# Attention and a mixture of experts on one core: GpSimd's drain alone ahead of the last branch, landings awaited inside the hand-ordered program, and the downward steps in another order

## The chip, the cores and the metric

The kernel runs on one core of a Trainium2 chip. The metric is the device time of one execution in microseconds (us). Before the change it is 524.77 us, the median of 3 runs (524.23 to 525.05). The core's engines are named as in the profile: PE (TensorE) does matmuls and transposes, DVE (VectorE) and ACT (ScalarE) do elementwise work and reductions, POOL (GpSimd) does some copies and generates the indirect DMAs, SP (SyncE) issues the other DMAs. PEld is PE's loading of weights, which overlaps its matmuls.

## What is computed

Attention, then a mixture of experts, on B = 4 sequences of S = 768 tokens with H = 8 heads of 64:

```python
keep = (pos < n_global) | ((rel >= 0) & (rel < n_local))     # 8 and 96
scores = where(keep, q @ k.T / 8 - slope[h] * dist, -1e9)
a = softmax(scores);  x = (a @ v) as 3072 rows of 512
logits = x @ w_gate;  expert = argmax(logits);  gate = softmax(logits)[expert]
for e in range(8):
    h = maximum(x[expert == e] @ w1[e], 0)                    # 512 x 1024
    out[expert == e] = gate * (h @ w2[e])                     # 1024 x 512
```

## The kernel before, in words

**One program in a written order.** Every operation is first recorded by a `Flow` in the order in which the code calls it. `derive` works out, per engine, which semaphores each operation has to wait for: an operation waits for the last writers of what it reads, for the readers of what it overwrites, and, in PSUM, bank by bank, for any other engine's last touch of that bank. `play` (L192) then emits all of it, engine by engine in the recorded order, as one block `tile_critical(name="flow")` (L207). There is no planner: the order of the calls is the order on each engine. Each DMA queue entry has a semaphore (`RINGS`); `play` collects their last levels in `landed`, and SP awaits them at the end of the block (L223-224). Stores to the output are left out of that (`later=outs`, in `rest`): they are awaited at the very end of the kernel (from L1668).

**Attention** (the first 170 us) runs over 24 blocks of 128 tokens. Each token's row, with its gate and its index, is scattered by GpSimd (L602) into a region of its expert in DRAM.

**The experts** (from 169.9 us) follow in the order 0, E, 1 to 7, by `group(p)`; E is a small extra region of tokens of expert 0 that came late. For each expert the tokens are padded to one of 17 widths (`SIZES`, 128 to 256 columns for half of the tokens); PE chooses the form of its code by a switch on a loaded index (`emit_forms`), by a branch (L260) that a hint some way ahead announces (L240). The two matrix products are each done in seven block products instead of eight: `up` is two times seven steps of 8 matmul records, `down` is seven steps of 16. A step of `down` takes 1.85 us in group 7 (136 columns) and up to 2.81 us in groups 1 and 5 (208 columns).

**The seven steps** are in `seven`. They use three PSUM banks X, Y and W out of `sets = ((0, 1, 2), (3, 4, 7))`, and the set changes with every call. `one` puts a product in X, and ACT copies it out as p1 (L833). `two` puts one in Y, and DVE adds it to p1 as u2 (L837). `three` adds a product to X and ACT takes c11 from it. `four` writes Y again, DVE makes u3 = u2 + Y (L848). `five` writes W and DVE makes c22 = u3 + W (L852); `six` writes Y and DVE makes c21 = u3 + Y (L857); `last` adds a product to W, and DVE makes c12 = u2 + W (L862). In `down` these four results are the quarters of the expert's output, transposed: c11 and c12 are blocks 0 and 2 of the tokens, c21 and c22 are blocks 1 and 3.

**Steps have numbers.** `up` has 0 to 13, `down` 14 (`D`) to 20. `at_(i, ...)` hangs other work behind the step number i: the sums of the next expert's weights (L683-686, `w_sums`) and inputs (L779, `x_in`), the issue of weight DMAs, the padding scatters (L728).

**The output of a group** is made by `y_out` (L790): four PE transposes into bank 6 or 5 (L794), a scale by the gate on ACT (L797) or on DVE (L799), and an indirect store that GpSimd generates (L800). It is called for the group before, between the first steps of `up`. Only the last group has none behind it: its four `y_out` (blocks 1, 3, 0, 2) come when all steps are done.

**The check and the end.** Behind the step D + 1 of the last group `check` (L1134) computes whether the inputs are such that this fast program is right: DVE reduces the sums of the softmax to one number per partition (L1139-1141), PE transposes it (L1143), DVE combines it with other conditions into `flag`. Behind the flow's block all engines load the flag (L1663) and branch on it (L1665): `anything` is a slow version for all inputs, and it isn't taken here. The flow's block ends with a drain of GpSimd, which stands in the trace at L207. `anything` has a wait of its own for the output stores (`again`).

Of the kernel before, what the change touches and what calls it, by code (L numbers as in the profile page):

```python
# [24 lines left out]
class Flow:  # L25
# [163 lines left out]
            op["clock"] = clock  # L189
        return procs  # L190

    def play(self, later=()):  # L192

        procs = self.derive()
        ops, tc = self.ops, self.tc
        sems = {p: tc.alloc_semaphore(f"{p[0].lower()}{'' if p[1] is None else p[1]}") for p in procs}
        level = {p: 0 for p in procs}
        landed, rest = {}, {}
        for op in ops:
            if op["dma"]:  # L200
                level[op["proc"]] += 16
                late = any(isinstance(t, str) and t in later for t in op["w"])
                (rest if late else landed)[op["proc"]] = level[op["proc"]]
            elif op.get("told"):
                level[op["proc"]] += 1
            op["level"] = level[op["proc"]]
        with tc.tile_critical(name="flow"):  # L207
            k = 0
            while k < len(ops):
                form = ops[k]["form"]  # L210
                if form is None:
                    self.emit(ops[k], sems, None)
                    k += 1
                    continue
                body = []
                while k < len(ops) and ops[k]["form"] is form:
                    if ops[k]["e"] == "PE":
                        body.append(ops[k])
                    else:
                        self.emit(ops[k], sems, None)  # L220
                    k += 1
                self.emit_forms(form, body, sems)
            for p, v in landed.items():  # L223
                self.nc.sync.wait_ge(sems[p], v)
        return [(sems[p], v) for p, v in rest.items()]

    def wait(self, op, sems):
        for j in op["need"]:
# [71 lines left out]
class Attention:  # L300
# [9 lines left out]
    GW, LW, P, E = 32, 97, 128, 8  # L310
# [299 lines left out]
class Experts:  # L610
# [9 lines left out]
    P, E, CAP, LATE = 128, 8, 512, 128  # L620
# [182 lines left out]
            _r=[k["to"][:, g, j:j + 1], self.y[j]], _w=[f"out{g}.{j}"])  # L803


    def product(self, bank, w, x, fresh):

        f, n = self.f, len(w)
        for t in range(2):
            for k in range(n):  # L810
                f.pe.matmul(self.psum[:, bank, 256 * t:256 * t + 256], lhsT=w[k][:, ts(t, 128)], rhs=x[k],  # L811
                            start=(fresh and t == 0 and k == 0), stop=True, skip_group_check=True, _dyn=True)

    def seven(self, c, a, s, cols, order, dst, act):

        f, V = self.f, self.f.dve
        X, Y, W = self.sets[self.turn]
        p1, u2, u3 = self.p1[self.turn], self.u2[self.turn], self.u3[self.turn]
        self.turn ^= 1

        def bank(b):
            return self.psum[:, b, :].rearrange("p (t c) -> p t c", t=2)

        def mm(b, wq, xq, fresh):
            self.product(b, [c[wq][:, k, cols] for k in order], [xq[:, k, :] for k in order], fresh)

        def relu(d):
            if act:
                f.act.activation(d, d, act)  # L829

        def one():
            mm(X, "b11", a["a11"], True)
            f.act.copy(p1, bank(X))  # L833

        def two():
            mm(Y, "t2", s[1], True)
            V.tensor_tensor(u2, p1, bank(Y), ALU.add)  # L837

        def three():
            mm(X, "b21", a["a12"], False)  # L840
            if act:
                f.act.activation(dst["c11"], bank(X), act)
            else:
                f.act.copy(dst["c11"], bank(X))

        def four():
            mm(Y, "t3", s[2], True)
            V.tensor_tensor(u3, u2, bank(Y), ALU.add)  # L848

        def five():  # L850
            mm(W, "t1", s[0], True)
            V.tensor_tensor(dst["c22"], u3, bank(W), ALU.add)  # L852
            relu(dst["c22"])

        def six():
            mm(Y, "t4", a["a22"], True)
            V.tensor_tensor(dst["c21"], u3, bank(Y), ALU.add)  # L857
            relu(dst["c21"])

        def last():  # L860
            mm(W, "b22", s[3], False)
            V.tensor_tensor(dst["c12"], u2, bank(W), ALU.add)  # L862
            relu(dst["c12"])

        return [one, two, three, four, five, six, last]

    def h_sums(self, j):
        V, sh = self.f.dve, self.sh
# [17 lines left out]
            steps += self.seven(c, a, s, slice(256 * j, 256 * j + 256), (0, 1), dst, AF.Relu)  # L886
        return steps

    def down(self, e):
        c, h, yt = self.quarters(e, False), self.h, self.yt  # L890
        a = dict(a11=h[:, 0:4, 0], a12=h[:, 4:8, 0], a21=h[:, 0:4, 1], a22=h[:, 4:8, 1])
        s = [self.sh[:, j] for j in range(4)]
        dst = dict(c11=yt[:, 0:2, 0], c12=yt[:, 2:4, 0], c21=yt[:, 0:2, 1], c22=yt[:, 2:4, 1])
        return self.seven(c, a, s, slice(0, 256), (0, 1, 2, 3), dst, None)


    def plain(self, e, slack):
# [23 lines left out]
def kernel(  # L921
# [12 lines left out]
    nc = tc.nc  # L934

    P = 128
    B, H, S, D = q.shape
    DM, E = moe_w_gate.shape
# [42 lines left out]
    with ExitStack() as stack:  # L981
# [149 lines left out]
        order = [0, E, *range(1, E)]  # L1131
        forms = [(keep["index"][0:1, g:g + 1], ex.SIZES, f"form{g}") for g in range(E)]

        def check():  # L1134


            ok, den = keep["ok"], keep["den"][:].rearrange("p n h -> p (n h)")
            for j, (src, op) in enumerate(((den, ALU.min), (den, ALU.max))):
                V.tensor_reduce(ok[:, j:j + 1], src, AX.X, op)  # L1139
            V.tensor_scalar(ok[:, 2:3], ok[:, 0:1], 0.125, None, ALU.is_ge)  # L1140
            V.scalar_tensor_tensor(ok[:, 3:4], ok[:, 1:2], 1.0e12, ok[:, 2:3], ALU.is_le, ALU.mult)
            row = psum[0:1, ex.tbanks[0], 0:P]
            f.pe.transpose(row, ok[:, 3:4], ident[:])  # L1143
            V.tensor_reduce(ok[0:1, 4:5], row, AX.X, ALU.min)
            V.tensor_reduce(ok[0:1, 0:1], keep["cnt"][0:1, :], AX.X, ALU.max)
            V.scalar_tensor_tensor(ok[0:1, 1:2], ok[0:1, 0:1], float(CAP), ok[0:1, 4:5], ALU.is_le, ALU.mult)
            V.scalar_tensor_tensor(ok[0:1, 2:3], keep["cnt"][0:1, E:E + 1], float(LATE), ok[0:1, 1:2], ALU.is_le,
                                   ALU.mult)
            V.scalar_tensor_tensor(ok[0:1, 5:6], ng[0:1], float(at.GW), ok[0:1, 2:3], ALU.is_le, ALU.mult)
            V.scalar_tensor_tensor(ok[0:1, 6:7], nl[0:1], float(at.LW), ok[0:1, 5:6], ALU.is_le, ALU.mult)  # L1150
            V.scalar_tensor_tensor(ok[0:1, 7:8], nl[0:1], 1.0, ok[0:1, 6:7], ALU.is_ge, ALU.mult)
            V.tensor_scalar(keep["flag"][0:1], ok[0:1, 7:8], -1.0, 1.0, ALU.mult, ALU.add)
# [16 lines left out]
        def group(p):  # L1169
# [6 lines left out]
            def at_(i, *fns):  # L1176
                todo.setdefault(i, []).extend(fns)
# [70 lines left out]
            else:  # L1248
                if nxt is not None:
                    sums, xs = ex.w_sums(nxt, True), ex.x_sums()  # L1250
                    at_(13, lambda: ex.x_in(nxt, 0))
                    at_(D + 1, lambda: ex.x_in(nxt, 1), sums[0])
                    at_(D + 3, xs[0], xs[1])
                    at_(D + 4, sums[1])
                    at_(D + 5, sums[2])
                    at_(D + 6, xs[2], xs[3], lambda: ex.marks(nxt))
                else:
                    at_(D + 1, check)
                if after is not None:
                    pieces = ex.w_pieces(after)  # L1260
                    at_(3, lambda: ex.pads(after))
# [5 lines left out]
                return  # L1267
            with f.forms(*forms[g]):
                run(ups[3:] if p else ups[2:], 3 if p else 2)
                run(ex.down(g), D)  # L1270
            assert not todo, todo

        for p in range(len(order)):
            group(p)
        for j, on in ((1, "act"), (3, "dve"), (0, "act"), (2, "dve")):
            ex.y_out(order[-1], j, on)
        outs = {f"out{g}.{j}" for g in range(E + 1) for j in range(1 if g == E else 4)}
        landing = f.play(later=outs)


    def anything(ctx):
        wpool = ctx.enter_context(tc.tile_pool(name="wpool", bufs=2))
        nc.scalar.dma_start(out=wg[:], in_=moe_w_gate.rearrange("(c p) e -> p c e", p=P))
        with tc.tile_critical(name="again"):
            for sem, level in landing:
                nc.gpsimd.wait_ge(sem, level)
            nc.gpsimd.iota(ebase[:], pattern=[[NTOK, E]], base=0, channel_multiplier=0,
                           allow_small_or_imprecise_dtypes=True)
        nc.vector.tensor_copy(out=base_e[:], in_=ebase[:])
        nc.gpsimd.iota(tokid[:], pattern=[[P, NBLK]], base=0, channel_multiplier=1)  # L1290

# [352 lines left out]
        with tc.manual_schedule(engines={PE}):  # L1644
# [5 lines left out]
            for j in range(JT):  # L1650
# [7 lines left out]
                if j + 2 < JT:  # L1658
                    fetch(j + 2)
            down(JT - 1)  # L1660


    redo = nc.values_load(keep["flag"][0:1, 0:1], min_val=0, max_val=1,  # L1663
                          skip_runtime_bounds_check_because="a comparison's result")
    with tc.If(redo > 0):  # L1665
        with ExitStack() as stack:
            anything(stack)
    with tc.tile_critical(name="landed"):  # L1668
        for sem, level in landing:
            nc.sync.wait_ge(sem, level)  # L1670


# [28 lines left out]
```

## Time and profile before

| what | us |
|---|---|
| median of 3 runs | 524.77 |
| the profiled execution's own time | 525.96 |
| its span, from the first instruction to the last | 524.1 |
| attention, up to the first step of the experts | 0 to 169.9 |
| last matmul step of the experts ends | 501.6 |
| end of the last generated store (L800) | 508.55 |
| its landing | 509.79 |
| GpSimd's drain | 505.63 to 515.25 |
| branches on the flag | 515.9 |

Busy time in four stretches of the span (us, PE's granted clock as a share of full speed):

| stretch | PE | DVE | ACT | POOL | clock |
|---|---|---|---|---|---|
| 0 to 165 | 147.74 | 110.47 | 91.09 | 95.59 | 0.98 |
| 240 to 480 | 237.57 | 173.25 | 57.51 | 47.51 | 1.00 |
| 480 to 510 | 20.95 | 16.55 | 5.29 | 3.89 | 0.97 |
| 510 to 524.1 | 0.00 | 0.00 | 0.00 | 0.00 | 0.50 |

An engine's row in the profile gives its busy time, the mean of one instruction, and the idle time ahead of it with what ended that. The chain of waits follows the work that ended last back to the beginning. DRAIN, COMPARE_BRANCH and EVENT_SEMAPHORE are records that don't count as busy; what lies behind 508.55 us consists of them and of DMAs.

### The profile page before, as it was taken

How to read it: one execution, taken by the hardware profiler on the slowest of the kernel's cores; microseconds unless marked ns; L12 is line 12 of the kernel's file. 1: busy time of each engine (PE TensorE's matmuls, PEld its weight loads, DVE VectorE, ACT ScalarE, POOL GpSimd, SP SyncE). 2: the span in 40 equal slices, each digit the busy share in tenths (PEclk: the TensorE clock that was granted, in tenths of full speed). 3: DMA queues.
4: the chain of work that ended last, by engine and by line, in shares of the span. 5: the costliest groups of instructions: out<-in, count | busy, mean ns of one | idle time of the engine just before them, and what ended most of it. 6: DMA issues, size and time to landing. Idle time of an engine off the chain costs nothing.

```text
span 524.1 us, 10715 instructions
## 1 busy us (share of the span) xinstructions
PE 480.1 (92%) x4397; PEld 451.6 (86%) x4397; DVE 349.4 (67%) x612; ACT 173.0 (33%) x290; POOL 168.5 (32%) x194
## 2 busy tenths in 40 slices
PE   4999999999968999999999999999998999999740
PEld 3788888888857999999999998999998999999740
DVE  4554765787885882747667866876865775777620
ACT  3765555656552222123033033023022113213210
POOL 1554465676675043240043042034032012002020
PEclk9999999999997999999999999999999999999985
DMA  9999999997325439996782880782891764001010
GB/s 153 205 246 248 177 218 258 224 226 187 88 89 115 161 135 210 207 282 124 179 224 73 202 223 29 159 237 80 189 258 53 161 197 112 1 3 63 1 44 8
DMA packets 120345, 79.25 MB, mean 151 GB/s; under 512 B 86422, under 2 KB 103318, under 8 KB 120272
## 3 DMA queue, kind: packets, MB, share of 16 engines
q1 hardware_dynamic: 112960, 63.77, 55.4%
q0 software_dynamic: 6480, 14.45, 7.7%
q8 instruction: 51, 0.84, 0.7%
q14 instruction: 22, 0.18, 0.1%
q10 hardware_dynamic: 832, 0.02, 0.1%
HBM read 61.39 MB, written 23.71 MB: 162 GB/s over the span
## 4 chain that ended last, share of the span: by engine, by line
PE 81%; DVE 7%; ACT 3%; POOL 2%; issue 2%; DMA 2%; POOLq 0%; SPq 0%; DVEq 0%; ACTq 0%
PE psum L811 55%; PE psum L466 6%; PE psum L503 6%; PE psum L904 3%; PE psum L794 2%; DVE arena L476 2%; PE psum L518 2%; PE psum L442 2%; PE psum L525 2%; PE psum L450 2%; DMA arena<-in_k_dram 2%; POOL xg_dram L602 1%; DVE arena L546 1%; ACT arena L444 1%; ACT arena L484 1%
## 5 line engine op out<-in xcount | busy, mean ns | idle before, releaser
L811 PE MATMUL psum<-arena 128*128 128x208 f32 (+5 forms) x1792 | 299.3, 328 | 2.6 <-ACT arena L833 2.4
L811 PEld LDWEIGHTS psum<-arena 128*128 128x128 f32 x1792 | 288.7, 190 | 8.6 <-ACT arena L833 3.3
L800 POOL DMA_INDIRECT out_dram<-arena,to x33 | 38.4, 1163 | 239.9 <-ACT arena L797 207.2
L476 DVE TENSOR_TENSOR arena<-psum,arena 128x1024 f32<-128x1024 f32 x40 | 48.8, 1219 | 37.7 <-PE psum L466 35.3
L490 POOL TENSOR_TENSOR arena<-arena 128x512 f32<-128x512 f32 x40 | 52.9, 1322 | 32.8 <-ACT arena L484 32.8
L484 ACT ACTIVATE arena<-arena 128x1024 f32<-128x1024 f32 (+1 forms) x48 | 47.4, 987 | 47.4 <-DVE arena L476 41.5
L466 PE MATMUL psum<-arena 64*128 64x128 f32 x704 | 50.1, 290 | 3.3 <-POOL arena L1035 1.4
L466 PEld LDWEIGHTS psum<-arena 64*128 64x128 f32 x704 | 44.6, 196 | 8.2 <-issue 3.7
L829 ACT ACTIVATE arena<-arena 128x512 f32<-128x512 f32 x48 | 30.2, 630 | 64.4 <-DVE arena L852 31.9
L503 PE MATMUL psum<-arena 128*64 128x128 f32 x704 | 44.6, 279 | 0.2 <-issue 0.2
L833 ACT COPY arena<-psum 128x512 f32<-128x512 f32 x24 | 14.0, 585 | 87.2 <-PE psum L811 87.1
L503 PEld LDWEIGHTS psum<-arena 128*64 128x64 f32 x704 | 38.8, 139 | 3.3 <-issue 0.6
L848 DVE TENSOR_TENSOR arena<-arena,psum 128x512 f32<-128x512 f32 x24 | 16.5, 688 | 29.9 <-PE psum L811 25.8
L602 POOL DMA_INDIRECT xg_dram<-arena,slot_i x24 | 27.0, 1126 | 21.2 <-DVE arena L862 15.8
L728 POOL DMA_INDIRECT xg_dram<-small,pad x24 | 26.3, 1098 | 12.5 <-issue 7.0
L797 ACT ACTIVATE arena<-psum,gt 128x512 f32<-128x512 f32 x31 | 19.8, 684 | 25.7 <-PE psum L794 25.7
L862 DVE TENSOR_TENSOR arena<-arena,psum 128x512 f32<-128x512 f32 x24 | 16.5, 688 | 17.5 <-PE psum L811 16.3
L852 DVE TENSOR_TENSOR arena<-arena,psum 128x512 f32<-128x512 f32 x24 | 16.5, 688 | 16.6 <-PE psum L811 15.2
L857 DVE TENSOR_TENSOR arena<-arena,psum 128x512 f32<-128x512 f32 x24 | 16.5, 688 | 14.7 <-PE psum L811 12.0
L837 DVE TENSOR_TENSOR arena<-arena,psum 128x512 f32<-128x512 f32 x24 | 16.4, 685 | 11.4 <-PE psum L811 10.3
L442 PE MATMUL psum<-ident,arena 128*128 128x128 f32 x96 | 15.5, 286 | 7.2 <-DMA arena<-in_k_dram 7.2
L779 DVE STREAM_TRANSPOSE arena<-arena 128x1024 f32<-128x1024 f32 (+1 forms) x17 | 20.3, 1203 | 2.7 <-PE psum L904 2.6
(139 smaller groups left out, 497.3 us busy)
## 6 DMA issues: line engine op xcount, KB each, us to landing
arena<-in_moe_w_dram SPq DMA_DIRECT2D x64, 512.0 KB
arena<-xg_dram SPq DMA_DIRECT2D x64, 128.0 KB
arena<-in_q_dram SPq DMA_DIRECT2D x24, 256.0 KB
arena<-in_k_dram SPq DMA_DIRECT2D x24, 256.0 KB
arena<-in_v_dram SPq DMA_DIRECT2D x24, 256.0 KB
xg_dram<-arena SPq DMA_DIRECT2D x2, 1032.0 KB
out_dram<-arena,to POOLq DMA_INDIRECT x33
xg_dram<-arena,slot_i POOLq DMA_INDIRECT x24
```

What stands on the lines that cost most here:

```text
L442: f.pe.transpose(pt[:, m, :], raw[:, 2 * m:2 * m + 2, :].rearrange("p a d -> p (a d)"), self.keep["ident"][:])
L466: f.pe.matmul(self.psum[:, 2 * g + a, c:c + P], lhsT=kt[r, m, :], rhs=qt[r, m, :], start=True, stop=True, skip_group_check=True)
L476: f.dve.tensor_tensor(e, s, self.bias[:, g, :, 1:3, :].rearrange("p h k c -> p h (k c)"), ALU.add)
L484: f.act.activation(e, e, AF.Exp)
L490: f.pool.tensor_tensor(self.es[n % 3][:, g], e[:, :, 0:P], e[:, :, P:2 * P], ALU.add)
L503: f.pe.matmul(po[r, m, :], lhsT=self.v[(n - ab) % 6][:, 2 * m + a, :], rhs=self.e[n % 2][:, m // 2, 2 * a + m % 2, P * ab:P * ab + P], sta ...
L602: self.f.pool.indirect_dma_start(out=self.xs[:], out_offset=bass.IndirectOffsetOnAxis(ap=k["slot_i"][:, b % 2, u:u + 1], axis=0), in_=self ...
L728: self.f.pool.indirect_dma_start(out=self.xs[:], out_offset=bass.IndirectOffsetOnAxis(ap=self.keep["pad"][:, g, j:j + 1], axis=0), in_=sel ...
L779: self.f.dve.transpose(out=self.xt[:, :, hh, 0:32 * nb].rearrange("p c (b t) -> p b c t", t=32), in_=self.x[g][:, hh, 0:nb])
L800: f.pool.indirect_dma_start(out=self.out[:], out_offset=bass.IndirectOffsetOnAxis(ap=k["to"][:, g, j:j + 1], axis=0), in_=self.y[j], in_of ...
L811: f.pe.matmul(self.psum[:, bank, 256 * t:256 * t + 256], lhsT=w[k][:, ts(t, 128)], rhs=x[k], start=(fresh and t == 0 and k == 0), stop=Tru ...
L829: f.act.activation(d, d, act)
```

## The change

- `play` no longer leaves out the output's stores: all landings are awaited by SP at the end of the flow's block, in the order in which the last DMAs of the semaphores were issued. The block is made with `no_gpsimd_drain=True`, and stands in a block of the program named "fast". The waits of `again` and `landed` are gone.
- Ahead of the flag's load stand a branch hint for all engines, placed there, and a drain of GpSimd alone (`nc.gpsimd.drain()`). The `If` has the false side as its fallthrough.
- `seven` takes a function `half`. If there is one, the steps come in the order one, two, four, five, six, three, last, and `three` calls it between its two halves (`product`). `group` hands a lambda to `down` in every group; its list `early` is empty but in the last group, where it holds blocks 1 and 3. Their `y_out` so comes in the middle of `three`, and blocks 0 and 2 follow at the end.
- `check` is cut in two: the four DVE operations on the sums (`check_sums`) stay behind step D + 1, the transpose and what follows it come behind step D + 3.

In the changed file the matmuls of the steps stand at L810 (L811 before), the add behind `two` at L838 (L837 before).

```diff
             op["clock"] = clock
         return procs
 
-    def play(self, later=()):
+    def play(self):
 
         procs = self.derive()
         ops, tc = self.ops, self.tc
         sems = {p: tc.alloc_semaphore(f"{p[0].lower()}{'' if p[1] is None else p[1]}") for p in procs}
         level = {p: 0 for p in procs}
-        landed, rest = {}, {}
+        landed = {}
         for op in ops:
             if op["dma"]:
                 level[op["proc"]] += 16
-                late = any(isinstance(t, str) and t in later for t in op["w"])
-                (rest if late else landed)[op["proc"]] = level[op["proc"]]
+                landed.pop(op["proc"], None)
+                landed[op["proc"]] = level[op["proc"]]
             elif op.get("told"):
                 level[op["proc"]] += 1
             op["level"] = level[op["proc"]]
-        with tc.tile_critical(name="flow"):
+        with tc.tile_critical(name="flow", no_gpsimd_drain=True):
             k = 0
             while k < len(ops):
                 form = ops[k]["form"]
...
                 self.emit_forms(form, body, sems)
             for p, v in landed.items():
                 self.nc.sync.wait_ge(sems[p], v)
-        return [(sems[p], v) for p, v in rest.items()]
 
     def wait(self, op, sems):
         for j in op["need"]:
...
             _r=[k["to"][:, g, j:j + 1], self.y[j]], _w=[f"out{g}.{j}"])
 
 
-    def product(self, bank, w, x, fresh):
+    def product(self, bank, w, x, fresh, half=None):
 
         f, n = self.f, len(w)
         for t in range(2):
             for k in range(n):
                 f.pe.matmul(self.psum[:, bank, 256 * t:256 * t + 256], lhsT=w[k][:, ts(t, 128)], rhs=x[k],
                             start=(fresh and t == 0 and k == 0), stop=True, skip_group_check=True, _dyn=True)
-
-    def seven(self, c, a, s, cols, order, dst, act):
+            if half and t == 0:
+                half()
+
+    def seven(self, c, a, s, cols, order, dst, act, half=None):
 
         f, V = self.f, self.f.dve
         X, Y, W = self.sets[self.turn]
...
         def bank(b):
             return self.psum[:, b, :].rearrange("p (t c) -> p t c", t=2)
 
-        def mm(b, wq, xq, fresh):
-            self.product(b, [c[wq][:, k, cols] for k in order], [xq[:, k, :] for k in order], fresh)
+        def mm(b, wq, xq, fresh, half=None):
+            self.product(b, [c[wq][:, k, cols] for k in order], [xq[:, k, :] for k in order], fresh, half)
 
         def relu(d):
             if act:
...
             V.tensor_tensor(u2, p1, bank(Y), ALU.add)
 
         def three():
-            mm(X, "b21", a["a12"], False)
+            mm(X, "b21", a["a12"], False, half)
             if act:
                 f.act.activation(dst["c11"], bank(X), act)
             else:
...
             V.tensor_tensor(dst["c12"], u2, bank(W), ALU.add)
             relu(dst["c12"])
 
-        return [one, two, three, four, five, six, last]
+        return [one, two, four, five, six, three, last] if half else [one, two, three, four, five, six, last]
 
     def h_sums(self, j):
         V, sh = self.f.dve, self.sh
...
             steps += self.seven(c, a, s, slice(256 * j, 256 * j + 256), (0, 1), dst, AF.Relu)
         return steps
 
-    def down(self, e):
+    def down(self, e, half=None):
+
         c, h, yt = self.quarters(e, False), self.h, self.yt
         a = dict(a11=h[:, 0:4, 0], a12=h[:, 4:8, 0], a21=h[:, 0:4, 1], a22=h[:, 4:8, 1])
         s = [self.sh[:, j] for j in range(4)]
         dst = dict(c11=yt[:, 0:2, 0], c12=yt[:, 2:4, 0], c21=yt[:, 0:2, 1], c22=yt[:, 2:4, 1])
-        return self.seven(c, a, s, slice(0, 256), (0, 1, 2, 3), dst, None)
+        return self.seven(c, a, s, slice(0, 256), (0, 1, 2, 3), dst, None, half)
 
 
     def plain(self, e, slack):
...
         order = [0, E, *range(1, E)]
         forms = [(keep["index"][0:1, g:g + 1], ex.SIZES, f"form{g}") for g in range(E)]
 
-        def check():
+        def check_sums():
 
 
             ok, den = keep["ok"], keep["den"][:].rearrange("p n h -> p (n h)")
...
                 V.tensor_reduce(ok[:, j:j + 1], src, AX.X, op)
             V.tensor_scalar(ok[:, 2:3], ok[:, 0:1], 0.125, None, ALU.is_ge)
             V.scalar_tensor_tensor(ok[:, 3:4], ok[:, 1:2], 1.0e12, ok[:, 2:3], ALU.is_le, ALU.mult)
+
+        def check():
+            ok = keep["ok"]
             row = psum[0:1, ex.tbanks[0], 0:P]
             f.pe.transpose(row, ok[:, 3:4], ident[:])
             V.tensor_reduce(ok[0:1, 4:5], row, AX.X, ALU.min)
...
                     at_(D + 5, sums[2])
                     at_(D + 6, xs[2], xs[3], lambda: ex.marks(nxt))
                 else:
-                    at_(D + 1, check)
+                    at_(D + 1, check_sums)
+                    at_(D + 3, check)
                 if after is not None:
                     pieces = ex.w_pieces(after)
                     at_(3, lambda: ex.pads(after))
...
                 return
             with f.forms(*forms[g]):
                 run(ups[3:] if p else ups[2:], 3 if p else 2)
-                run(ex.down(g), D)
+                early = ((1, "act"), (3, "dve")) if nxt is None else ()
+                run(ex.down(g, lambda: [ex.y_out(g, j, on) for j, on in early]), D)
             assert not todo, todo
 
         for p in range(len(order)):
             group(p)
-        for j, on in ((1, "act"), (3, "dve"), (0, "act"), (2, "dve")):
+        for j, on in ((0, "act"), (2, "dve")):
             ex.y_out(order[-1], j, on)
-        outs = {f"out{g}.{j}" for g in range(E + 1) for j in range(1 if g == E else 4)}
-        landing = f.play(later=outs)
+        with tc.block(name="fast"):
+            f.play()
 
 
     def anything(ctx):
         wpool = ctx.enter_context(tc.tile_pool(name="wpool", bufs=2))
         nc.scalar.dma_start(out=wg[:], in_=moe_w_gate.rearrange("(c p) e -> p c e", p=P))
-        with tc.tile_critical(name="again"):
-            for sem, level in landing:
-                nc.gpsimd.wait_ge(sem, level)
-            nc.gpsimd.iota(ebase[:], pattern=[[NTOK, E]], base=0, channel_multiplier=0,
-                           allow_small_or_imprecise_dtypes=True)
+        nc.gpsimd.iota(ebase[:], pattern=[[NTOK, E]], base=0, channel_multiplier=0,
+                       allow_small_or_imprecise_dtypes=True)
         nc.vector.tensor_copy(out=base_e[:], in_=ebase[:])
         nc.gpsimd.iota(tokid[:], pattern=[[P, NBLK]], base=0, channel_multiplier=1)
 
...
             down(JT - 1)
 
 
+    tc.mark_branch_hint_location("redo", "LikelyTaken", list(mybir.ALL_ENGINES))
+    nc.gpsimd.drain()
     redo = nc.values_load(keep["flag"][0:1, 0:1], min_val=0, max_val=1,
                           skip_runtime_bounds_check_because="a comparison's result")
-    with tc.If(redo > 0):
+    with tc.If(redo > 0, preferred_fallthrough_block=True, label="redo"):
         with ExitStack() as stack:
             anything(stack)
-    with tc.tile_critical(name="landed"):
-        for sem, level in landing:
-            nc.sync.wait_ge(sem, level)
 
 
 # ---- launch: one core; inputs and outputs as the reference has them ----
```

## The prediction, made before the run

> **What bounds the kernel now.** I read the page's busy shares and its chain first, to see which engine carries the end; then the timeline of one turn between two downward steps; then the waits of the last 45 us; then the records behind the last transfer.
>
> ```profile
> PE 480.1 (92%) x4397; PEld 451.6 (86%) x4397; DVE 349.4 (67%) x612; ACT 173.0 (33%) x290; POOL 168.5 (32%) x194
> ...
> PE 81%; DVE 7%; ACT 3%; POOL 2%; issue 2%; DMA 2%; POOLq 0%; SPq 0%; DVEq 0%; ACTq 0%
> ...
> L811 PE MATMUL psum<-arena 128*128 128x208 f32 (+5 forms) x1792 | 299.3, 328 | 2.6 <-ACT arena L833 2.4
> ```
>
> PE is the path: 81% of the chain, and ahead of 1792 matmuls of L811 it idles 2.6 us in all. Whatever stops PE between two of these matmuls is paid in full. Now one turn, group 5 (PE, then DVE):
>
> ```profile
> 411.68 8.60 PE L811 MATMUL psum<-arena 128*128 128x208 f32 x48
> ```
>
> ```profile
> 412.83 0.69 DVE L837 TENSOR_TENSOR arena<-arena,psum 128x512 f32<-128x512 f32 x1 [0.72 <-PE psum L811]
> 413.44 1.22 DVE L686 TENSOR_TENSOR arena<-arena 128x1024 f32<-128x1024 f32 x1
> ```
>
> 48 matmuls run without a break, one every 0.176 us. Step `two` ends in them, and `three` starts at 412.56. DVE adds bank Y (L837) from 412.83 to 413.52, while PE is in bank X with `three`. In the last group PE does stop, at the check's transpose:
>
> ```profile
> PE psum L1143 <- DVE ok L1141: 2.8, 1, 2.8
> ```
>
> And the end: the four stores, and the records of lines 207 and 1665 (engine op xcount: minimum/median/maximum ns).
>
> ```profile
> 503.75 0.97 POOL L800 DMA_INDIRECT out_dram<-arena,to  x1 [27.29 <-DVE arena L799]
> ...
> 507.58 0.97 POOL L800 DMA_INDIRECT out_dram<-arena,to  x1 [0.30 <-issue]
> ```
>
> ```profile
> L207 POOLq DRAIN  x1: 9620/9620/9620, 505.6 to 505.6; - x1
> ```
>
> ```profile
> L1665 SPq EVENT_SEMAPHORE  x9: 17/17/17, 519.4 to 519.9; - x9
> ...
> L1665 PEldq COMPARE_BRANCH  x1: 4603/4603/4603, 515.7 to 515.7; - x1
> ```
>
> The last store is generated by E = 508.55 (507.58 + 0.97) and recorded as landed at 509.79. GpSimd's drain ends at 515.25; only then do the engines load the flag (0.5 us) and branch (515.9). Their next records stand at 519.1 to 520.4. The end is at 524.1: 15.55 us behind E.
>
> **Part 1, the turned order, groups 0 to 6.** `down` hands `half` to every group, and a lambda is always true, so all eight groups get the order one, two, four, five, six, three, last. That moves `three` (bank X, 16 matmul records) behind `six`, and puts `four` right behind `two`. Both write bank Y, and `four` waits for L837's read of it. Today `three` covers this read; then nothing does. In group 5 PE would go on at 412.56, L837 ends at 413.52, and a PE that waited for L837 started 0.05 behind its end at 481.50 (480.77 + 0.68 = 481.45). That is 1.01 us; the second matmul behind such a wait comes some 0.1 late (0.22 instead of 0.116 at 481.50). So 1.1 us. Groups 1 to 6 all show the same 1.01 from their own rows: 6 x 1.1 = 6.6. In group 0 the add stands behind twelve table operations (L1125 to L740) and ends at 196.68, where `three` starts at 194.83: 1.9 + 0.1 = 2.0. Sum **+8.6**. From below 0 per turn, if a write could enter the bank beside the read; from above the 2.76 of the longest PE wait on DVE. I take 1.1, since both ends of this wait are rows of the same instructions.
>
> What follows loses nothing: behind L837, DVE has L686, L779 and L683 queued (to 4.4 us after `two`), so `four`'s add comes late at 5.1, but `six`, which needs it, starts at 1.1 + 2 x 2.5 = 6.1 in the groups of 184 columns. `last` needs `five`'s add, done long before. The DMAs issued at these places (the w1 pieces behind `one`, the w2 pieces behind `last`) keep them; at the same distance to PE, they land a group ahead.
>
> [...]
>
> **Part 2, the last group.** Before, PE stands from 489.28 to 492.20 for the check. After, `check_sums` stays there on DVE, and the transpose comes behind `five`, when its operand is ready. `four` starts with L837's end, 489.54 + 0.69 + 0.05 = 490.28. Then: `four`, `five` (1.85 us each, plus 0.1) to 494.1; transpose 0.1; `six` to 496.05. DVE does the check's eight small operations (1.43, from 492.50 to 493.93 before) behind `five`'s add and so adds c21 at 496.45 to 497.15. Half of `three` to 496.98, a wait of 0.2, transposes for blocks 1 and 3 (0.44 each and 0.1) to 498.2, the other half to 499.1, `last` to 500.95. Blocks 1 and 3 are stored by 501.8, beside it. c12 is added to 501.84; block 0 transposed, scaled (0.69) to 503.16, its store starts 0.79 later as at 503.75 (502.96 before), and two stores at 0.97 and a gap of 0.30 end at 506.2. Before: 508.55. **-2.4**, bounds -1.9 and -2.9 by the order of DVE's small operations.
>
> **Part 3, behind E.** After: landing 1.24. SP awaits it as its last waits, signals, and GpSimd passes a no-op and the hint: 0.5 by the hops between records at 521.80 and 522.19. Then the drain, d. Then the flag load 0.50, the branch 0.06, a hinted branch's 0.3 (median of PE's hinted branches, L260), GpSimd's part of the false block 0.72 (519.47 to 520.19), a drain 0.18, and the final barrier 1.16 (522.96 to its end). Sum d + 4.66. SP's block of 23 waits for landings (520.07 to 521.96) is gone; SP has 3 us less to do than GpSimd. The other engines branch while GpSimd drains.
>
> d is not shown for a GpSimd whose stores have landed. The record of 9.62 starts while two stores are still to be generated, so it holds 6.70 behind E, or 5.46 behind the landing. From below: the drains of L1696, 0.18, where no transfer came since the last drain. From above: 9.62. I take 6.1, between the two readings of the same row, which is nearest. The end is then E + 10.76 in place of E + 15.55: **-4.8**.
>
> [...] The rows have SP's branch at 515.90 and its next record 3.4 us later. [...]
>
> **Sum.** 8.6 - 2.4 - 4.8 = +1.4 on the profiled execution: span 524.1 to 525.5, its own time 525.96 to 527.4. That execution lies 1.2 above the median of the runs, so the change is put on the median: 524.77 + 1.4 = **526.2**.
>
> **Rivals.**
> - *The drain finds everything landed and is short.* It then starts 1.74 behind E, with nothing to wait for. For it: 0.18 at L1696. Against: 5.46 us passed behind the landing in this trace. It decides from d below 4.7, where the change stops being slower; below 3.5 the code of the false block is last (hint at E + 1.7, 3.4 for the code, 1.4 for SP's waits, 0.3, 1.2: E + 8.1, saved 7.45). 8.6 - 2.4 - 7.45 = -1.2: **523.5** to 524.8.
> [...]
> - *The turn costs half or less*, because PE's queue of loaded weights or an earlier add covers it. Against: L837 starts with PE's end in groups 1 to 6 (`[0.72 <-PE`). 8.6 becomes 4.3: **521.9**. The change would then be what the last group's rows promise.
> - The drain takes 9.62 from its own start: +3.5, **529.7**; little speaks for it, as two stores lie inside.
>
> **How the numbers follow.** Likeliest case 0.50, own range 525.2 to 527.3 (d from 5.46 to 6.70 gives 525.5 to 526.8, part 2 and the turn add 0.3 on each side, rounded up). Short drain 0.22, hint 0.12, half turn 0.12, long drain 0.04. The range holds the first three: 523.4 to 529.4. A measurement of this kernel can tell about 0.2%, 1.05 us, from no change. Slower by more: 0.65 of the likeliest, the hint and the long drain, 0.48. Within: 0.35 of the likeliest and three quarters of the short drain, 0.34. Faster: the rest of the short drain and the half turn, 0.18.
>
> **What would show it.** In groups 1 to 6 a PE wait of some 1.0 us for L838 (L837's new line) ahead of one L810 step, seven in all with group 0's 1.9; PE's idle time ahead of L810 near 11 us in place of 2.6; no PE wait of 2.8 at the check; E some 6 us later in the span (8.6 - 2.4); the GpSimd drain alone, about 6 us, starting 0.5 behind the last landing; COMPARE_BRANCH at the flag short on all engines and their next records within 0.5 us. Seven stalls that aren't there, or a drain under 3 us, would make the forecast wrong.

## The result, and the profile after

The changed kernel takes 527.62 us (median of 4 runs, 527.18 to 528.74), the kernel before 524.50 (4 runs): the ratio is 1.0076, with a 95% interval of 1.0055 to 1.0097. The change makes the kernel slower, by 3.1 us between the medians. The profiled execution took 527.18 us, with a span of 525.4 (before 525.96 and 524.1).

From the page of the changed kernel: the busy times, the chain's shares by engine, and the group of the steps' matmuls, whose last column is PE's idle time ahead of them.

```profile
PE 481.2 (92%) x4397; PEld 451.8 (86%) x4397; DVE 349.0 (66%) x612; ACT 172.9 (33%) x290; POOL 170.8 (33%) x194
...
PE 78%; DVE 10%; ACT 3%; issue 2%; POOL 2%; DMA 1%; SPq 0%; DVEq 0%; POOLq 0%; ACTq 0%
...
L810 PE MATMUL psum<-arena 128*128 128x208 f32 (+5 forms) x1792 | 300.7, 328 | 7.9 <-DVE arena L838 7.7
```

PE does the same work in about the same time (481.2 us busy, 480.1 before). What is new is DVE in its chain (10% in place of 7%) and 7.7 us of waiting for one DVE line. PE's waits of the changed kernel name it (us in total, times, longest):

```profile
PE psum L810 <- DVE arena L838: 7.7, 8, 1.7
```

Eight waits, one in each group. In group 5, PE and then DVE:

```profile
409.80 5.97 PE L810 MATMUL psum<-arena 128*128 128x208 f32 x33
416.61 9.59 PE L810 MATMUL psum<-arena 128*128 128x208 f32 x53 [0.85 <-DVE arena L838]
```

```profile
415.87 0.69 DVE L838 TENSOR_TENSOR arena<-arena,psum 128x512 f32<-128x512 f32 x1 [0.72 <-PE psum L810]
```

Where 48 matmuls ran without a break before, PE now stops: `two` begins at 412.78 and would be followed at 415.59 (2.81 later); `four` starts at 416.61, 0.05 behind the end of the add. That is 1.01 more from start to start (3.828 in place of 2.814, unrounded); the profile's 0.85 is less because it counts from the modelled end of the last matmul.

The end, by GpSimd's last store and by the records of lines 1668 and 1671:

```profile
510.27 0.98 POOL L799 DMA_INDIRECT out_dram<-arena,to  x1 [0.30 <-issue]
```

```profile
L1668 POOLq DRAIN  x1: 6680/6680/6680, 512.9 to 512.9; - x1
```

```profile
L1671 SPq EVENT_SEMAPHORE  x9: 17/17/17, 517.0 to 517.6; - x9
L1671 POOLq EVENT_SEMAPHORE  x5: 17/43/43, 522.8 to 523.2; - x5
L1671 PEldq COMPARE_BRANCH  x1: 4006/4006/4006, 513.5 to 513.5; - x1
...
L1671 SPq COMPARE_BRANCH  x1: 75/75/75, 513.8 to 513.8; - x1
...
L1671 POOLq COMPARE_BRANCH  x1: 79/79/79, 520.2 to 520.2; - x1
```

The drain takes 6.68. The four other engines pass their branches beside it, and GpSimd branches at 520.25, when everybody else is done. Its next record comes at 522.85, 2.60 later, in spite of the hint at 512.84.

**Where the time went, in the two profiled executions.** I followed the start of each step:

| stretch | us |
|---|---|
| start of the experts | -0.16 |
| seven turns: 1.9 + 6 x 1.01 and 7 late second matmuls of 0.1 | +8.66 |
| two waits of PE for ACT's copy (L833) that the execution before had | -2.98 |
| other small ones | -0.25 |
| so `down` of group 7 starts (485.50 to 490.77) | +5.27 |
| from there to the end of the last generated store, E (23.05 to 20.48) | -2.57 |
| from E to the end of the span (15.55 to 14.15) | -1.40 |
| span (524.1 to 525.4) | +1.30 |

The third row is not an effect of the change, as far as the traces show. In the execution before, ACT's copy behind `one` began late at two places (318.18 and 399.16, the first 1.74 us behind the end of PE's step), and PE waited for it; the traces of e3 and e9 below, which keep the order of the kernel before, have no such wait either. Without this row the sum is +4.3. The medians lie +3.1 apart, which would fit fewer such waits in other executions of the kernel before; that isn't shown, since only one of them was traced.

### The profile page after: what moved, and what is told of

Its sections match the earlier page's. It is cut to its first block, busy times and chain, and to the rows that moved or that the text cites. A ratio compares the mean times of both kernels' runs of the same rounds, so it can differ in the third digit from the quotient of the medians.

```text
span 525.4 us, 10700 instructions
## 1 busy us (share of the span) xinstructions
PE 481.2 (92%) x4397; PEld 451.8 (86%) x4397; DVE 349.0 (66%) x612; ACT 172.9 (33%) x290; POOL 170.8 (33%) x194
## 4 chain that ended last, share of the span: by engine, by line
PE 78%; DVE 10%; ACT 3%; issue 2%; POOL 2%; DMA 1%; SPq 0%; DVEq 0%; POOLq 0%; ACTq 0%
PE psum L810 53%; PE psum L465 7%; PE psum L502 6%; PE psum L906 3%; PE psum L793 3%; DVE arena L475 2%; PE psum L517 2%; PE psum L441 2%; PE psum L524 2%; PE psum L449 2%; POOL xg_dram L601 1%; DMA arena<-in_k_dram 1%; DVE arena L838 1%; DVE arena L545 1%; DVE arena L863 1%
## 5 line engine op out<-in xcount | busy, mean ns | idle before, releaser
L810 PE MATMUL psum<-arena 128*128 128x208 f32 (+5 forms) x1792 | 300.7, 328 | 7.9 <-DVE arena L838 7.7
L810 PEld LDWEIGHTS psum<-arena 128*128 128x128 f32 x1792 | 288.9, 190 | 15.0 <-DVE arena L838 10.2
L799 POOL DMA_INDIRECT out_dram<-arena,to x33 | 39.9, 1210 | 240.8 <-ACT arena L796 211.5
L845 ACT COPY arena<-psum 128x512 f32<-128x512 f32 x8 | 4.7, 586 | 97.3 <-PE psum L810 97.3
L834 ACT COPY arena<-psum 128x512 f32<-128x512 f32 x24 | 14.0, 584 | 35.9 <-PE psum L810 35.8
L838 DVE TENSOR_TENSOR arena<-arena,psum 128x512 f32<-128x512 f32 x24 | 16.4, 685 | 9.2 <-PE psum L810 8.7
```

The costliest lines, as they stand in the source:

```text
L799: f.pool.indirect_dma_start(out=self.out[:], out_offset=bass.IndirectOffsetOnAxis(ap=k["to"][:, g, j:j + 1], axis=0), in_=self.y[j], in_of ...
```

## The experiments

Each kernel was measured beside the kernel before on the same chip; that one took 523.6 us beside the first four, 523.2 beside the next four, 523.3 beside the three after these and 527.0 beside the last.

**e1_turn_last: the new order in the last group alone.**

```diff
-                run(ex.down(g, lambda: [ex.y_out(g, j, on) for j, on in early]), D)
+                half = (lambda: [ex.y_out(g, j, on) for j, on in early]) if early else None
+                run(ex.down(g, half), D)
```

> The changed kernel with the new order of the downward steps in the last group alone; groups 0 to 6 keep one, two, three, four, five, six, last. Theory: the exposed reads of bank Y (L838) cost 1.9 + 0.1 in group 0 and 1.01 + 0.1 in each of groups 1 to 6, 8.6 in all, so 527.6 - 8.6 = 519.0; seven of the eight PE waits for L838 are gone and one of 1.0 stays. Rival: the stalls are paid back later (in the trace the lag to the kernel before falls from 3.9 to 2.6 and from 4.7 to 3.0 behind the first steps of two groups), so undoing them brings only what is left of them, 8.6 - 2.8 = 5.8: 521.8.

Measured: 518.69 us, ratio 0.9900 (0.9873 to 0.9928). PE's waits in its profile:

```profile
PE psum L810 <- DVE arena L838: 0.8, 1, 0.8
```

One wait is left of eight. The time is 8.9 under the changed kernel's median, or 8.0 if the 0.9 by which the kernel before was faster on this chip is taken off; 8.6 was expected, and the rival had 5.8: the stalls are not paid back. With this one condition the change is a gain.

**e2_swap_banks: the turned order, with banks Y and W exchanged from `four` on.**

```diff
+        V4, V5 = (W, Y) if half else (Y, W)
...
         def four():
-            mm(Y, "t3", s[2], True)
+            mm(V4, "t3", s[2], True)
...
         def five():
-            mm(W, "t1", s[0], True)
+            mm(V5, "t1", s[0], True)
```

(`six` uses V4 and `last` V5 in the same way, and so do the adds that read them.)

> The changed kernel with its new order in all groups, but in the turned order four and six write bank W, and five and last bank Y, so that no step writes a bank just behind its reading. Theory (the wait is for the bank): all eight waits are gone, 527.6 - 8.6 - 1.1 = 517.9. Rival (four would be late anyway, by its operands or by the late u3 in DVE's queue): 525 to 527.6 with waits of PE at other lines.

Measured: 517.74 us, ratio 0.9891 (0.9862 to 0.9919). The group of the steps' matmuls:

```profile
L810 PE MATMUL psum<-arena 128*128 128x208 f32 (+5 forms) x1792 | 298.9, 328 | 0.5 <-DVE arena L785 0.4
```

All eight groups are turned and no wait for L838 is left. What PE waited for was the bank, not operands or a late u3. The order itself costs nothing.

**e3_end_only: the new end alone.** `down(g)` without `half`, one `check` behind step D + 1, and the outputs 1, 3, 0, 2 at the end, as before the change.

> The new end alone (landings inside the flow, hints, the drain of GpSimd alone), all downward steps, the check and the four last outputs as before the change. Theory from the trace of the changed kernel: from the end of the last generated store to the end of the span 14.15 in place of 15.55, so 524.5 - 1.4 = 523.1. The forecast on record had 4.8 for it: 519.7. Rival: the end brings nothing or costs, as its drain starts behind the landing: 524.5 to 526.

Measured: 522.95 us, ratio 0.9974 (0.9956 to 0.9991). In its trace 14.15 us pass from E to the end, in place of 15.55: a gain of 1.4, not of 4.8. The ratio gives 1.4 too (0.0026 x 523.6), the medians 0.7. The 12 runs lie in two bunches, five from 521.08 to 522.01 and seven from 522.91 to 523.50; the profiled one (521.28) has 0.2 us of idle time ahead of L810. What separates the bunches isn't shown: none of the upper one was traced.

**e4_no_hints: e1 without its hints.**

```diff
-    tc.mark_branch_hint_location("redo", "LikelyTaken", list(mybir.ALL_ENGINES))
```

> The kernel e1_turn_last without the branch hints. Theory (the hints fetch nothing: no instruction DMA between them at 512.8 and the first branch at 513.5, and GpSimd's at 521.3 comes 1.0 behind its branch): the same time as e1_turn_last within 0.3. Rival (a hint saves 0.5 to 1 of the 3.2 us from SP's branch to its next record in the kernel before): 0.5 to 1 slower than e1_turn_last, with 3.2 us or more between GpSimd's branch and its next record in place of 2.6.

Measured: 519.16 us, ratio 0.9904 (0.9877 to 0.9932), against 0.9900 for e1. GpSimd's records at the flag, of e1 and then of e4:

```profile
L1672 POOLq EVENT_SEMAPHORE  x5: 17/43/43, 514.5 to 514.9; - x5
...
L1672 POOLq COMPARE_BRANCH  x1: 79/79/79, 511.6 to 511.6; - x1
```

```profile
L1671 POOLq EVENT_SEMAPHORE  x5: 17/43/43, 515.5 to 515.9; - x5
...
L1671 POOLq COMPARE_BRANCH  x1: 59/59/59, 512.7 to 512.7; - x1
```

2.9 us from the branch to the next record, with the hint 7.4 us ahead of the branch and without one. The medians differ by 0.47, less than the intervals; by the traces, E to the end is 14.42 with hints and 14.31 without.

**What the drain's price is: e5 to e8 and e11**, all of them e2 with GpSimd's drain put elsewhere.

```diff
# e5: one more drain, in the last group
-                    at_(D + 1, check_sums)
+                    at_(D + 1, check_sums, lambda: f.pool.drain())
# e6: in the flow, right behind the last store, in place of the one ahead of the branch
+        f.pool.drain()
# e7: none
-    nc.gpsimd.drain()
# e8: two in a row
+    nc.gpsimd.drain()
# e11: one more, in group 4
+                    if g == 4:
+                        at_(D + 1, lambda: f.pool.drain())
```

> The kernel e2_swap_banks with one more drain of GpSimd, in the last group, where GpSimd stands idle ahead of its last four stores (some 12 us). Theory A: a drain's 6.68 us count what GpSimd issued since the drain before (81 indirect DMAs, 0.08 each); then the early drain takes 6.4 in idle time and the last one, with 4 stores behind it, 0.3 to 0.7. The end is then set by the other engines' code behind the branch (PE's next record at 508.8 in e2_swap_banks): 517.7 - 5.2 = 512.5. Theory B: 6.68 is the price of any drain that finds indirect DMAs issued: two drains of 6.68, time as e2_swap_banks, 517.7.

Measured: 512.61 us, ratio 0.9801 (0.9785 to 0.9818). The added drain and the last one:

```profile
L1265 POOLq DRAIN  x1: 9405/9405/9405, 470.8 to 470.8; - x1
```

```profile
L1670 POOLq DRAIN  x1: 385/385/385, 503.1 to 503.1; - x1
```

0.39 in place of 6.68, by a drain that runs while GpSimd has nothing else to do (its record begins while two stores are still ahead of it; it ends at 480.25, and the next store is at 494.76). Theory A holds.

> The kernel e2_swap_banks with GpSimd's drain right behind its last store, inside the flow, beside the landings that SP awaits. Theory (the drain doesn't wait for landings, it takes 6.68 from where it starts; in the kernel before it ended 6.70 behind the last store's end): it starts at 501.8 in place of 503.46, so 517.7 - 1.7 = 516.0. Rival (it waits for the landings too, or takes longer beside them): 517.0 to 517.7.

Measured: 517.67 us, ratio 0.9903 (0.9878 to 0.9928). The drain:

```profile
L1286 POOLq DRAIN  x1: 8610/8610/8610, 500.3 to 500.3; - x1
```

The last store ends at 502.18 and the drain at 508.87, 6.69 later: it doesn't wait for the landings first (the last one is at 503.42), as the theory had it. But no time is won. All five engines now branch at 509.4 to 509.7, GpSimd's next record comes 3.57 behind its branch, and PE's at 514.0 is later still. The price of the four other engines' branches, hidden beside the drain until then, is what ends last. The number was the rival's, the mechanism wasn't.

> The kernel e2_swap_banks without the drain ahead of the branch; all landings are still awaited by SP. Theory: the price goes to the next drain of GpSimd, the one at the program's end (0.04 in e2_swap_banks): GpSimd branches at 504.1, has its code at 506.8 and ends the drain at 513.8, where it stood at 514.04: 517.7 - 0.3 = 517.4. Rival (awaited landings leave nothing to drain): the end is set by the other engines' code, 512.5.

Measured: 518.67 us, ratio 0.9915 (0.9899 to 0.9932). The drains at the program's end:

```profile
L1700 POOLq DRAIN  x3: 40/188/6687, 508.9 to 516.5; - x3
```

One of the three now takes 6.69. All landings had been awaited 6 us earlier, so the drain's price isn't waiting for transfers. The time is 1.3 above the theory's 517.4: the five engines branch together, and GpSimd's next record comes 3.58 behind its branch, not 2.7.

> The kernel e2_swap_banks with two drains of GpSimd in a row ahead of the branch. Theories A and B: the second has nothing issued since the first and takes 0.2 or less: 517.9. Rival (any drain there has 6.68): 524.4.

Measured: 517.89 us, ratio 0.9900 (0.9880 to 0.9920). The second drain of the two:

```profile
L1671 POOLq DRAIN  x1: 34/34/34, 510.3 to 510.3; - x1
```

It finds nothing issued since the first and takes 0.03. The rival, 6.68 for any drain at this place, is out.

> The kernel e2_swap_banks with its second drain in group 4, behind step D + 1: 20 indirect DMAs come behind it, 61 ahead. Theory (0.082 each and 0.06): the last drain takes 1.7, the time is 513.0 to 513.4. Rival (the price is by what lies in the queue, gone with time): 0.4 as in e5_drain_twice, where 4 came behind it: 512.6.

Measured: 512.75 us, ratio 0.9797 (0.9779 to 0.9815). The added drain and the last one:

```profile
L1261 POOLq DRAIN  x1: 12150/12150/12150, 351.9 to 351.9; - x1
```

```profile
L1672 POOLq DRAIN  x1: 1692/1692/1692, 503.2 to 503.2; - x1
```

Behind 0, 4, 20 and 81 indirect DMAs a drain takes 0.03, 0.39, 1.69 and 6.68 us: 0.082 for each and 0.06 more, and the 20 were foretold from the 4 and the 81. The drains in the middle fit too, counted from the end of the last store issued before they end: 5.06 behind it for 61 (e11) and 6.36 for 77 (e5). All these DMAs have 128 rows, so whether DMAs or rows are counted is not told apart. The medians of few runs (2 and 4) lie 0.1 apart, below the theory's 513.0 and near the rival's 512.6, and don't decide; the drain's record does, and by the traces E to the end is 9.6 in place of 8.7.

**e9_before_drain: the kernel before, with one drain more.**

```diff
-                    at_(D + 1, check)
+                    at_(D + 1, check, lambda: f.pool.drain())
```

> The kernel before the change with one line more: a drain of GpSimd in the last group, behind step D + 1, where GpSimd has nothing to do. Theory (a drain's price is 0.08 us for each indirect DMA since the drain before): the drain at the flow's end takes 0.4 behind the last store's end (508.55) in place of 6.70, and nothing else moves: 523.4 - 6.3 = 517.1, more than the whole change was to bring at its end. Rival (the branches then meet the last landing, or the code comes later): 518.5 to 520.

Measured: 520.35 us, ratio 0.9935 (0.9922 to 0.9949): half of the 6.3. The flow's drain and GpSimd's records at the flag:

```profile
L207 POOLq DRAIN  x1: 4387/4387/4387, 503.3 to 503.3; - x1
```

```profile
L1665 POOLq EVENT_SEMAPHORE  x6: 17/30/43, 512.0 to 512.5; - x6
L1665 POOLq COMPARE_BRANCH  x1: 55/55/55, 508.4 to 508.4; - x1
L1665 POOLq INC_SWDGE_SEM  x1: 176/176/176, 515.5 to 515.5; - x1
```

Two things took the rest, together somewhat more than the 3.3 that are missing. The drain ends at 507.73, 1.45 behind E and 0.21 behind the last landing (the same 1.45 and 0.21 in e10): behind 4 stores, with the last one still out, it seems to wait for the landing, 1.1 more than the 0.39 of e5. And GpSimd's INC_SWDGE_SEM comes 3.0 behind its last semaphore (512.5 to 515.5), where it followed at once before (519.9 to 520.0); SP's waits stand behind it. What GpSimd stood for in these 3 us the trace doesn't say.

**e10_old_end: e5 with the end of the kernel before** (its `play`, its `landed`, no hints, no drain ahead of the branch).

> The kernel e5_drain_twice with the end of the kernel before: landings of the output awaited behind the branch, GpSimd's drain in the flow's exit, no hints. Theory: last store's end 501.4, drain to 501.9, branches at 502.5, and 8.2 from there to the end as before the change (515.9 to 524.1): 510.7 against the 510.1 of e5_drain_twice, so 513.2: of the change's end 0.6 is left. Rival (the landings' 1.7 us, now beside the code's loading, win): 511.0 to 512.0.

Measured: 515.98 us, ratio 0.9867 (0.9851 to 0.9882), against 0.9801 for e5. Both theories fail: the new end is worth 3.4 us here, not 0.6 or less than nothing. GpSimd's and the other branches come at the same time (503.8 and 504.1 in e5), but GpSimd's INC_SWDGE_SEM comes at 510.19 in place of 508.01 (the gap of e9 again, 2.3), and from there to the end 3.4 pass in place of 2.1, because SP walks through its waits twice, in the block `landed` and behind it (at the program's end the kernel before has 36 of SP's semaphore records, the changed one 14).

**e12_best_no_hints: e5 without hints.**

> The kernel e5_drain_twice (turned order with exchanged banks, drain in the last group's idle time) without the branch hints. Theory (hints fetch nothing here): 512.6 within 0.4, from GpSimd's branch to its next record 3.4 us as with them. Rival (with the drain short, the five engines branch together and a hint shortens that): 1 us or more slower.

Measured: 515.26 us beside 526.95 for the kernel before on that chip, ratio 0.9770 (0.9743 to 0.9797). From GpSimd's branch to its next record 3.41 us, with hints 3.44; from the drain's start to the end 7.0 with and without. The time is 2.7 above the expected 512.6, but on this chip the kernel before takes 3.7 more than beside e5; by the ratios the version without hints is 0.3% faster, and the intervals overlap. No effect of the hints is to be seen here. e5, e11 and e12 are the fastest versions, 2.0 to 2.3% under the kernel before.

## Why the prediction was right, and where it was wrong

The side and the range were right, and the sum of +1.4 stands beside a span that grew by 1.3. That agreement is partly luck: one term was off by 3.4 us and the late copies of the execution before hid 3.0 of it. Between the medians the change cost 3.1 (the interval of the ratio: 2.9 to 5.1), and 527.62 lies 1.4 above the forecast and 0.3 above the likeliest case's own range.

- **Part 1, +8.6: right**, mechanism and size. The trace has the 1.9 and six times 1.01 that were read off DVE's rows of the kernel before; e1 gives 8.0 to 8.9 for the seven turns, and e2, where `four` writes W while DVE reads Y, shows that it is the bank: of the 7.7 us of waits for L838 none is left. PE's idle time ahead of L810 was 7.9, not the forecast's 11: the 2.4 for ACT's copies stayed away, and the profile counts 0.85 for each 1.01.
- **The rival of the half turn** is out: no cover was found in any group.
- **Part 2, -2.4: right.** -2.57 in the trace. `four` starts at 495.55, the check's transpose at 499.36 and E is 511.25; the prediction's times plus the 5.27 that the kernel had lost by then are 495.55, 499.37 and 511.47. The medians are less clear: e1 and e3 differ by the last group alone and lie 4.3 apart, their traces only 2.4, and e3's trace is from its lower bunch.
- **Part 3, -4.8: mis-sized; it was -1.4.** E to the end was put at d + 4.66 = 10.76 and is 14.15. Term by term: the drain starts 1.69 behind E (1.74 expected); d is 6.68 (6.1); load and branch 0.64 (0.56); from the branch to the next record 2.60 (0.3); the rest 2.55 (2.06). So the failed step is the price of "a hinted branch's 0.3", 2.3 of the 3.4: it was taken from PE's hinted branches in the middle of the kernel, and e4 and e12 show no effect of the hints ahead of this branch. The sign that all branches would be short and followed by a record within 0.5 us failed with it: PE's took 4.0, and the others' next records came 2.6 to 3.3 behind them. What the chances call the hint (0.12, and with it the range's upper end of 529.4) is nearest to this: the hints ahead of this branch had no effect to be seen, and 2.3 us passed that the forecast didn't have.
- **d, 0.6 of the 3.4.** It lay between two readings of one row, 5.46 behind the landing and 6.70 behind E. The second was the price itself: the drain didn't wait for the landing and then take 5.46; it took 0.082 for each of 81 indirect DMAs, from where it started (6.68 here and in e2), or from the end of the last store where that was later (6.70 in the kernel before, 6.69 in e6). This also says what the prediction missed most: putting the drain behind the landings makes it start 1.7 later for nothing, though e6 shows that moving it ahead again wins nothing as long as the other engines' branches wait for it. The long drain's 9.62 is out with the 6.68.
- **The short drain's rival** is out for this kernel, since no drain was made between. But e5 shows that its time was there to be had, by a drain earlier (0.39 is left of 6.68), not by landed transfers. From E to the end 8.7 pass there, near the 8.1 that this rival had.

The time behind the branch holds transfers of instructions. GpSimd's branch in the changed kernel (520.25) is followed by one piece of 8 KB on the instruction queue q14 from 521.3 to 521.6, 1.0 behind it, and by its next record at 522.85. Between the hint at 512.84 and the branch that queue moved three pieces of 8 KB from 514.6 on and three from 517.3 on, as many as the engines ACT, DVE and SP, which had branched at 513.6 to 513.8. That none was for GpSimd is read from this count and from the piece behind its own branch; that GpSimd waited for that piece is a reading of these times and wasn't shown otherwise.

**Left open:** why GpSimd stands 2.3 to 3.0 us ahead of INC_SWDGE_SEM in e9 and e10; why ACT's copy begins late in some executions; and why PE's hinted switches in the middle have branches of 0.3 to 2.3 us (L259 of the changed kernel) and its branch at the end has 4.0: no kernel without the hints in the middle was run, and an earlier hint at the end wasn't tried.

## What to carry to other kernels

Before two steps are brought together, look for the step between them that hides a read of the bank: here the reader's end minus the writer's new start was the price (1.01 us in each of six groups), and exchanging the free bank for the read one left none of the 7.7 us of waits (e2). A condition that is meant for one group (a callback that is always true) is to be read as the program reads it. At the end of a kernel ask how many indirect DMAs GpSimd's drain has behind it (0.082 us for each here), and let it run in idle time, ahead of the last transfers (e5: 0.39 us is left of 6.68).

## What the runs showed of the hardware

- GpSimd's drain took 0.39, 1.69 and 6.68 us behind 4, 20 and 81 indirect DMAs (of 128 rows) issued since its last drain (e5, e11, e2), with all of them landed: 0.082 for each and 0.06 more. Behind none it took 0.03 (e8). Behind 4, with the last transfer still out, it ended 0.2 behind the last landing (e9, e10).
- A drain that was left out moved its price to the next one (6.69 at the program's end in e7, where the drains of the changed kernel take at most 0.19).
- From GpSimd's branch at the kernel's end to its next record 2.6 to 2.9 us passed where GpSimd branched alone (changed kernel, e1, e4), 3.4 to 3.6 where five engines branched together (e5, e6, e12); PE's branch record took 3.6 (e1) to 4.6 (the kernel before).
